# Attention and two expert layers on one core: first batch with S placed by a mask on VectorE, the queries behind the keys, the sums over 64 value columns, and the first slot's products by token halves

## The chip, the cores and the metric

The kernel runs on 1 core of one Trainium2 chip. The metric is the time of one execution in device microseconds (us), taken as the median of several runs. The engines are TensorE (PE; its weight loads are listed apart as PEld), VectorE (DVE), ScalarE (ACT), GpSimd (POOL), and SyncE (SP), which issues nearly all transfers. Each engine works through its own instructions strictly in order. An instruction waits until its operands are written and until the place it writes to has been read, and everything behind it on the same engine waits with it.

## What is computed

The reference, cut to what matters (4 batches, 4 heads, 1088 tokens, 32 values per head):

```python
def phi(x):                                   # 8 x 8 = 64 features of a row
    a = np.einsum('rd,bhsd->bhsr', S1, x)
    b = np.einsum('rd,bhsd->bhsr', S2, x)
    return np.einsum('bhsi,bhsj->bhsij', a, b).reshape(*x.shape[:-1], r * r)
q_p, k_p = phi(q), phi(k)
kv = np.einsum('bhsf,bhsd->bhfd', k_p, v);  z = np.sum(k_p, axis=2)
num = np.einsum('bhsf,bhfd->bhsd', q_p, kv)
den = np.einsum('bhsf,bhf->bhs', q_p, z)[..., None] + 1e-06
x = num / den                                 # 4352 tokens of 128
xn = x / rms * rms_g
g = xn @ w_gate                               # 128 -> 1536
x = (g / (1 + exp(-g)) * (xn @ w_val)) @ w_out
# then a soft mixture of 8 experts over all tokens: exp of x @ phi,
# sums over the tokens, 8 two-layer experts on 4 slots each, and back
```

The weights of the first expert layer and S1, S2 arrive as 64-bit floats; the kernel makes 32-bit words of them on the chip.

## The kernel before

**Stages.** A *front* works on batch 0 alone until the first 512 tokens (tile 0) are ready. Then 102 *slots* follow: tiles 0 to 7 have 512 tokens and 12 slots each, one for each 128 columns of the 1536; tile 8 has 6. The second expert layer and the way back make the end. Beside the slots run the key chains of batches 1 to 3, the query chain of the next tile and, in the first slots, the conversion of the weights.

**The front.** `FRONT` (L31 to L35) is an order written out by hand: each token names a step, and `in_order` (L872) holds each step's instructions behind the earlier ones of the same engine. The tokens that matter here:
- `n:18` and so on: fillers on TensorE (`keep_busy`, L301), products of a constant tile `hot` that nothing reads.
- `b`: `make_bd` (L260) makes words of S1 and S2 (tile `w4`, four copies side by side, by an add on POOL, L207), turns them with one TensorE transpose (L268), and copies the four blocks to the block diagonal `bd` with four ACT copies (L270). `bd` is the moving operand of every projection.
- `kt:0`, `kt:1`: key transposes on DVE, two halves each (L341). `kp`: projections of the keys (L359). `kt:2`, `kc:2`, `kp:2`: the same for the last 64 tokens.
- `qs`, `qp`: the query transpose on DVE (L506) and the query projection (L511), standing between the keys' first and last steps.
- `kx`, `ko`: the two halves of a projection are taken out of PSUM on ACT (L282, L279), and their outer products made on DVE or POOL (L287).
- `kv`: the values go to `va`, 33 columns a head with a column of ones (L352, ACT).
- `ks`: the sums over the tokens (L389): for each pair of heads a *bank* of 18 products with 33 columns of `va` as weights, which gives the rows 0 to 32 and 64 to 96 of a PSUM bank.
- `kw`: two copies of 33 rows for each bank to `kvT` (L407), spread four times; the rows between were zeroed once (L168). `kb`: transposes of it (L417). `kl`: placing them in `kvz` (L434). `qa` and after: attention, division, scaling by the root (L534 to L588), the transpose of the tokens (L594), and `xh` and `xl`, high and low part, by halves of 256 tokens (L601, L607).
- `c:0`, `c:1`, `c:2`: the next step of the conversion of a piece of the weights. Pieces 0, 1, 3, 4, 6 and 7 hold 256 columns each of gate and value weights and serve two slots; pieces 2, 5 and 8 hold output weights. The steps of a piece: absolute value (ACT, L192), shift (DVE, L194), low part (ACT, L198), join (DVE, L200), add (POOL, L204, two halves); then the high part `wgh` (ACT, L242) and the low part `wgl` (POOL, L249, two halves; of piece 0 on DVE, L251).

**A slot.** `ff_in` makes gate `g` and value `v` for 128 columns, each from three products of 512 tokens (`xh` by `wgh`, `xl` by `wgh`, `xh` by `wgl`; L647, L649, L648 in `mm3`). ACT takes silu of `g` (L677), DVE multiplies by `v` (L678, to `hh` in tile 0), and two slots later `ff_out` adds the product with the output weights to `o` (L702). `g` and `v` have two PSUM buffers each, so a slot waits until the slot two before it was read. The order within the slots is set by the scheduler of the language by its own costs, not by hand. `gate` holds the name of a product of the newest slot; transfers of the next batch wait for it.

## Time and profile before

| what | us |
|---|---|
| three runs, median (lowest, highest) | 316.48 (315.41, 316.87) |
| the profiled execution | 315.62 |
| its span, first to last instruction | 313.8 |
| outside the span | 1.82 |
| PE busy | 305.0 (97%) |
| DVE, ACT, POOL busy | 234.2, 181.4, 62.7 |

The page of the profile gives busy times over the whole span. An engine's share there says little of a change at one place, so the rows below come from the first 35 us. Fillers count as busy.

### The profile page before, as it was taken

The page shows a single profiled execution, that of the slowest core. Times are in us where ns is not written, and L with a number is a line of the kernel's source. Part 1 is how long each engine was busy: PE and PEld are TensorE (multiplying, and loading weights), DVE is VectorE, ACT ScalarE, POOL GpSimd, SP SyncE. Part 2 cuts the span into 40 slices and gives each one's busy share as a digit, 9 for nine tenths or more (in the row PEclk, how much of TensorE's full clock was granted, in tenths as well). Part 3 has the DMA queues.
Part 4 walks back from the last instruction along what each step waited for, and adds up shares of the span by engine and source line. Part 5 has one row for each costly group of instructions (what it writes and reads, how often), then busy time and mean ns, then how long its engine had stood idle before and what let it go on. Part 6 is the DMA issues. An engine that isn't in the chain of part 4 may idle for free.

```text
span 313.8 us, 5571 instructions
## 1 busy us (share of the span) xinstructions
PE 305.0 (97%) x1987; PEld 243.0 (77%) x1987; DVE 234.2 (75%) x454; ACT 181.4 (58%) x411; POOL 62.7 (20%) x104
## 2 busy tenths in 40 slices
PE   8989999999999999999999999999999999999993
PEld 6776676778888878888888788888787778898473
DVE  3787976688789858967798689678787667664673
ACT  3768674456645467555644676555574655567542
POOL 3347999000521010020010100100020100003030
PEclk9999999999999999999999999999999999999999
DMA  7998000010026100010261000100891493000007
GB/s 194 282 337 214 1 0 1 10 23 4 0 85 138 25 2 0 9 26 0 84 140 22 3 0 10 25 0 11 293 260 26 140 301 95 2 0 2 3 3 282
DMA packets 44955, 23.97 MB, mean 76 GB/s; under 512 B 26880, under 2 KB 40960, under 8 KB 44928
## 3 DMA queue, kind: packets, MB, share of 16 engines
q1 hardware_dynamic: 44752, 23.56, 27.7%
q8 instruction: 15, 0.25, 0.3%
q10 hardware_dynamic: 176, 0.07, 0.1%
q14 instruction: 12, 0.10, 0.1%
HBM read 19.81 MB, written 2.23 MB: 70 GB/s over the span
## 4 chain that ended last, share of the span: by engine, by line
PE 89%; DVE 2%; SPq 2%; POOL 2%; DMA 1%; issue 1%; ACT 1%; DVEq 0%; POOLq 0%; ACTq 0%
PE v L647 8%; PE g L647 8%; PE g L649 8%; PE g L648 7%; PE v L648 7%; PE v L649 7%; PE o L649 7%; PE o L647 7%; PE o L648 7%; PE aux L534 4%; PE o L702 3%; PE aux L389 2%; SPq L76 2%; PE aux L359 2%; PE aux L511 2%; PE fo L1207 1%
## 5 line engine op out<-in xcount | busy, mean ns | idle before, releaser
L677 ACT ACTIVATE silu<-g 128x512 f32<-128x512 f32 (+1 forms) x103 | 60.6, 593 | 38.0 <-PE g L649 37.3
L687 ACT CAST hh<-hf 128x512 fp32r<-128x512 f32 x89 | 54.8, 617 | 45.3 <-DVE hf L678 43.5
L678 DVE TENSOR_TENSOR hf<-v,silu 128x512 f32<-128x512 f32 (+1 forms) x91 | 61.1, 677 | 23.3 <-ACT hh L687 7.8
L692 DVE TENSOR_TENSOR hl<-hf,hh 128x512 fp32r<-128x512 f32 x89 | 61.0, 687 | 13.6 <-ACT hh L687 12.5
L647 PE MATMUL g<-xh,wgh 128*128 128x512 f32 (+1 forms) x108 | 43.8, 407 | 1.0 <-ACT xh L601 0.6
L647 PE MATMUL v<-xh,wgh 128*128 128x512 f32 (+1 forms) x108 | 43.4, 402 | 0.0
L648 PE MATMUL g<-xh,wgl 128*128 128x512 f32 (+1 forms) x108 | 41.1, 380 | 0.5 <-POOL wgl L249 0.5
L649 PE MATMUL g<-xl,wgh 128*128 128x512 f32 (+1 forms) x108 | 41.5, 384 | 0.0
L648 PE MATMUL v<-xh,wgl 128*128 128x512 f32 (+1 forms) x108 | 41.4, 383 | 0.0
L649 PE MATMUL v<-xl,wgh 128*128 128x512 f32 (+1 forms) x108 | 40.9, 379 | 0.0
L647 PE MATMUL o<-hh,woh 128*128 128x512 f32 (+1 forms) x94 | 36.9, 393 | 0.0
L649 PE MATMUL o<-hl,woh 128*128 128x512 f32 (+1 forms) x94 | 36.8, 392 | 0.0
L648 PE MATMUL o<-hh,wol 128*128 128x512 f32 (+1 forms) x94 | 35.8, 381 | 0.0
L582 POOL TENSOR_SCALAR rs<-ss 128x4 f32<-128x4 f32 (+1 forms) x8 | 1.9, 241 | 143.0 <-ACT sq L575 142.9
L647 PEld LDWEIGHTS g<-xh,wgh 128*128 128x128 f32 x108 | 20.4, 189 | 6.6 <-ACT silu L677 1.5
L648 PEld LDWEIGHTS g<-xh,wgl 128*128 128x128 f32 x108 | 20.3, 188 | 4.9 <-POOL wgl L249 0.9
L647 PEld LDWEIGHTS v<-xh,wgh 128*128 128x128 f32 x108 | 20.4, 188 | 4.3 <-issue 1.1
L649 PEld LDWEIGHTS g<-xl,wgh 128*128 128x128 f32 x108 | 20.3, 188 | 4.0
L648 PEld LDWEIGHTS v<-xh,wgl 128*128 128x128 f32 x108 | 20.4, 189 | 3.9 <-issue 0.7
L649 PEld LDWEIGHTS v<-xl,wgh 128*128 128x128 f32 x108 | 20.3, 188 | 3.9 <-issue 0.2
L649 PEld LDWEIGHTS o<-hl,woh 128*128 128x128 f32 x94 | 17.7, 188 | 3.7 <-issue 0.8
L647 PEld LDWEIGHTS o<-hh,woh 128*128 128x128 f32 x94 | 17.7, 188 | 3.4 <-issue 0.4
(263 smaller groups left out, 512.4 us busy)
## 6 DMA issues: line engine op xcount, KB each, us to landing
ring<-in_moe_w_dram SPq DMA_DIRECT2D x12, 256.0 KB, 6.9
ring<-in_moe_w_dram SPq DMA_DIRECT2D x5, 512.0 KB, 5.2
ring<-in_k_dram SPq DMA_DIRECT2D x8, 256.0 KB, 3.0
qt<-in_q_dram SPq DMA_DIRECT2D x4, 512.0 KB, 5.4
ring<-in_v_dram SPq DMA_DIRECT2D x16, 128.0 KB, 4.8
ring<-in_moe_w_gate_dram SPq DMA_DIRECT2D x6, 256.0 KB, 5.7
ring<-in_moe_w_val_dram SPq DMA_DIRECT2D x6, 256.0 KB, 7.1
ring<-in_moe_w_out_dram SPq DMA_DIRECT2D x3, 512.0 KB, 7.3
```

Source lines behind the costliest of these rows:

```text
L76: i = (on or nc.sync).dma_start(out=out, in_=in_)
L359: pe.matmul(o, self.kT[g][:, P * t : P * t + pp], bdf, start=True, stop=True)
L389: pe.matmul(self.a["kv", hp][64 * h2 : 64 * h2 + D1, 64 * hp : 64 * hp + 64], va[:, h, 2 * i + g, :] if t < 8 else vr[:, h, :], self.pk[hp ...
L534: pe.matmul(o, pD[:, f, h, :], rhs, start=(f == 0), stop=(f == 1))
L647: first = pe.matmul(o, ah, bh, start=start, stop=False)
L648: pe.matmul(o, al, bh, start=False, stop=False)
L649: last = pe.matmul(o, ah, bl, start=False, stop=stop)
L677: mark["silu"] = act.activation(s[:, cs], g[:, cs], AF.Silu).ins
L678: mark["gate"] = mark["gate", T, f] = dve.tensor_tensor(out=hf32[T, f][:, cs], in0=v[:, cs], in1=s[:, cs], op=ALU.mult).ins
L687: act.copy(hh[T, f], hf32[T, f])
L692: dve.tensor_tensor(out=hl[T, f], in0=hf32.pop((T, f)), in1=hh[T, f].bitcast(F32), op=ALU.subtract)
L702: last = pe.matmul(ops[T][:, 0:w], w_c, h[:, cs], start=(c == 0), stop=(c == NF - 1))
```

## The change

- **Placing S.** The four-fold `w4` is gone; the add of this step is made on DVE. Four TensorE products with the identity put the turned S into the four quarters of a PSUM tile. A new step `bm` (`place_bd`) multiplies it, read four times over, by a mask `blk` into all of `bd` in one DVE instruction. It stands between the two halves of `kt:0`. POOL makes the mask (five small memsets) in place of zeroing `bd`.
- **Order of the front.** `kp:2` is ahead of `qs` and `qp`; three fillers and two conversion steps ahead of the sums' results move: the low part of piece 0 (`c:0`, ACT) goes behind `kl`, and its `wgl` on DVE ahead of the scaling (`qm`).
- **Sums over 64 columns.** The weights of a sum are 64 columns of `va` (which gets a tail of 31 zeros) in place of 33. So the rows 0 to 127 of the bank are written, and one copy of 97 rows takes the place of two of 33, in the front and in the later batches; zeroing `kvT` is gone.
- **The first slot.** Its products with `xh` are made for tokens 0 to 255 first (high and low weights, `g` and `v`), then for 256 to 511, then both products with `xl` whole. `gate` keeps the first product of this slot.

```diff
-n:18 b n:5 kz kt:0 kt:1 qs kp:0 kp:1 kt:2 kx:0:a ko:0:d kx:1:b ko:1:p kc:2 qp kp:2 n:3 kv:0 kx:2:a ko:2:d qh kv:1 km
-ks:0 c:0 qo:0 qo:1 qb c:0 c:0 ks:1 kw:0:a kb:0 kw:1:a n:4 kb:1 n:10 kl:0:a kl:1:d c:0 c:0 kr:a c:1
-qa:0 qa:1 n:26 qd:0 qd:1 c:0 qq:0:a qq:1:d qq:2:a qq:3:d qr:0 qr:1 c:1 qm:0 qm:1 c:1 c:0 qt:0 qx:0 n:2 qt:1 qx:1 c:1 ql c:1 c:2 c:2 c:2
+n:18 b n:5 kz kt:0:0 bm kt:0:1 kt:1 kp:0 kp:1 kt:2 kx:0:a ko:0:d kx:1:b ko:1:p kc:2 kp:2 qs qp kv:0 kx:2:a ko:2:d qh kv:1 km
+ks:0 c:0 qo:0 qo:1 qb c:0 ks:1 kw:0:a kb:0 kw:1:a n:4 kb:1 n:10 kl:0:a kl:1:d c:0 c:0 c:0 kr:a c:1
+qa:0 qa:1 n:26 qd:0 qd:1 c:0 qq:0:a qq:1:d qq:2:a qq:3:d qr:0 qr:1 c:0 qm:0 qm:1 c:1 c:1 qt:0 qx:0 n:2 qt:1 qx:1 c:1 ql c:1 c:2 c:2 c:2
...
-        if len(out.shape) == 2:
+        if out.shape[1] == D:
+            dve.tensor_tensor(out=out, in0=s, in1=r, op=ALU.add)
...
-        pe.transpose(a[:, 0 : 2 * R], w4.rearrange("p h d -> p (h d)"), ident[0 : 2 * R, 0 : 2 * R])
-        for h in range(4):
-            act.copy(bd[32 * h : 32 * h + 32, h, :], a[32 * h : 32 * h + 32, 0 : 2 * R])
+        for h in range(H):
+            pe.matmul(a[32 * h : 32 * h + 32, 0 : 2 * R], w, ident[0 : 2 * R, 0 : 2 * R], start=True, stop=True)
+        kt["S"] = a
+
+    def place_bd():
+        a = kt.pop("S")[:, 0 : 2 * R].unsqueeze(1).to_broadcast([P, H, 2 * R])
+        dve.tensor_tensor(out=bd, in0=a, in1=blk.unsqueeze(2).to_broadcast([P, H, 2 * R]), op=ALU.mult)
...
-                        self.a["kv", hp][64 * h2 : 64 * h2 + D1, 64 * hp : 64 * hp + 64],
-                        va[:, h, 2 * i + g, :] if t < 8 else vr[:, h, :],
+                        self.a["kv", hp][64 * h2 : 64 * h2 + 64, 64 * hp : 64 * hp + 64],
+                        (va_all if t < 8 else vr_all)[:, v0 : v0 + 64],
...
-            for h2 in range(2):
-                r0 = 64 * h2
-                src = self.a["kv", hp][r0 : r0 + D1, 64 * hp : 64 * hp + 64].rearrange("p (a n) -> p a n", n=D)
-                eng(kvT[r0 : r0 + D1, 2 * hp : 2 * hp + 2], src.unsqueeze(2).to_broadcast([D1, 2, 4, D]))
+            src = self.a["kv", hp][0:97, 64 * hp : 64 * hp + 64].rearrange("p (a n) -> p a n", n=D)
+            eng(kvT[:, 2 * hp : 2 * hp + 2], src.unsqueeze(2).to_broadcast([97, 2, 4, D]))
...
+        if (T, f) == (0, 0):
+            os, sl = (gps[T, f][0], vps[T, f][0]), slice(0, P)
+            for cs in cuts(512):
+                for w_m in (wgh, wgl):
+                    for m, o in enumerate(os):
+                        last = pe.matmul(o[:, cs], w_m[:, m, sl], xh[T][:, cs], start=(w_m is wgh and cs.start == 0), stop=False)
+                        gate[0] = gate[0] or last.ins.name
+            for m, o in enumerate(os):
+                last = pe.matmul(o, wgh[:, m, sl], xl[T], start=False, stop=True)
```

The line numbers in the orders of after are those of the changed file (L198, L204, L206, L212 are the conversion steps L192, L198, L200, L204 of before).

TensorE, from the key projections to the sums. Before (`x_192` is the transposed queries, `T` the transposed keys; each filler has a load of `hot` and a product):

```order
L344 MATMUL v<-ident,kr 128x64
L511 MATMUL aux<-bd,x_192 128x64 x4
L359 MATMUL g<-bd,T 64x64
L301 LDWEIGHTS hot
L301 MATMUL idle<-hot 128x256
...
L389 MATMUL v<-work,va 33x64 x16
L389 MATMUL v<-pkr,vr 33x64 x2
```

After:

```order
L353 MATMUL v<-ident,kr 128x64
L368 MATMUL aux<-bd,T 64x64
L517 MATMUL g<-bd,x_220 128x64 x4
L399 MATMUL v<-work,va 64x64 x16
L399 MATMUL v<-pkr,vr 64x64 x2
```

The query projection now stands directly ahead of the sums, and the fillers there are gone.

ACT, after the low part of piece 1 (of the weights of slots 2 and 3) in the first slots. Before:

```order
L601 ACTIVATE xh<-v,g_sb 128x256
L192 ACTIVATE ring<-ring 128x512
L198 ACTIVATE cvc<-ring 128x512
L242 CAST wgh<-cvt 128x2x256
L677 ACTIVATE silu<-g 128x512
L192 ACTIVATE hf<-ring 128x512
L198 ACTIVATE cvc<-ring 128x512
L192 ACTIVATE hf<-ring 128x512
L677 ACTIVATE silu<-g 128x512 x2
```

After:

```order
L607 ACTIVATE xh<-v,g_sb 128x256
L198 ACTIVATE ring<-ring 128x512
L204 ACTIVATE cvc<-ring 128x512
L694 ACTIVATE silu<-g 128x512
L198 ACTIVATE hf<-ring 128x512 x2
L247 CAST wgh<-cvt 128x2x256
L204 ACTIVATE cvc<-ring 128x512
L694 ACTIVATE silu<-g 128x512
```

The cast that slot 2 needs moved behind the first silu and two absolute values of later pieces.

POOL, the conversion in the first slots (`cvt` is piece 1, `ring` output weights, `hf` pieces 3 and 4). Before:

```order
L204 TENSOR_TENSOR cvt<-cvs,cvc 128x256 x2
L249 TENSOR_TENSOR wgl<-cvt,wgh 128x256 x2
L204 TENSOR_TENSOR ring<-cvs,cvc 128x256 x2
L204 TENSOR_TENSOR hf<-cvs,cvc 128x256 x4
L249 TENSOR_TENSOR wgl<-hf,wgh 128x256 x4
```

After:

```order
L212 TENSOR_TENSOR cvt<-cvs,cvc 128x256 x2
L212 TENSOR_TENSOR ring<-cvs,cvc 128x256 x2
L254 TENSOR_TENSOR wgl<-cvt,wgh 128x256 x2
L212 TENSOR_TENSOR hf<-cvs,cvc 128x256 x4
L254 TENSOR_TENSOR wgl<-hf,wgh 128x256 x2
L212 TENSOR_TENSOR ring<-cvs,cvc 128x256 x2
L254 TENSOR_TENSOR wgl<-hf,wgh 128x256 x2
```

The output weights went ahead of the low part that slots 2 and 3 need.

## Rows read from the trace of the kernel before

**Rows 1.** Windows: length, then busy us (instructions) of each engine, granted clock, DMA.

```profile
22.65:34.20 11.55, 10.60 (x42) 6.79 (x42) 9.77 (x18) 9.23 (x18) 9.22 (x12) 1.00 0.62 152
34.20:290.00 255.80, 255.80 (x1569) 207.70 (x1573) 196.74 (x361) 149.03 (x331) 41.36 (x66) 1.00 0.21 53
```

**Rows 2.** Timeline of PE, 5 us: start, duration, engine, line, tiles, count.

```profile
5.17 0.28 PE L268 MATMUL aux<-ident,csr 16*128 16x16 f32 x1
5.39 1.24 PE L301 MATMUL idle<-hot 128*128 128x256 bf16 x5
6.43 0.25 PE L359 MATMUL aux<-bd,T 128*128 128x64 f32 x1
```

**Rows 3.** Timeline of ACT in the front; in brackets the idle time before.

```profile
5.49 0.69 ACT L270 COPY bd<-aux 32x16 f32<-32x16 f32 x4 [1.31 <-PE aux L268]
7.50 0.27 ACT L282 COPY asb<-aux 128x128 f32<-128x128 f32 x1 [1.32 <-PE aux L359]
...
12.07 0.66 ACT L198 ACTIVATE cvc<-ring 128x512 uint32<-128x512 uint32 x1
...
13.39 0.74 ACT L407 COPY kvT<-aux 33x256 f32<-33x256 f32 x2
```

**Rows 4.** Timeline of DVE in the front: key transposes, query transpose, first outer product.

```profile
4.41 2.01 DVE L341 STREAM_TRANSPOSE T<-ring 128x256 f32<-128x256 f32 x4
7.48 0.71 DVE L506 STREAM_TRANSPOSE x<-qt 128x512 f32<-128x512 f32 x1 [1.06 <-DMA qt<-in_q_dram]
8.12 1.18 DVE L287 TENSOR_TENSOR work<-asb,aux 128x1024 f32<-128x1024 f32 x1
```

**Rows 5.** Timeline of PE: query projection and the two banks of sums.

```profile
8.49 1.10 PE L511 MATMUL aux<-bd,x 128*128 128x64 f32 x8
...
10.22 1.09 PE L389 MATMUL v<-work,va 128*33 128x64 f32 x32
...
12.49 0.30 PE L389 MATMUL aux<-pkr,vr 64*33 64x64 f32 x4
```

**Rows 6.** Groups by line and form, weight loads: busy us, mean ns, idle before.

```profile
L389 PEld LDWEIGHTS aux<-work,va 128*33 128x33 f32 x224 | 6.5, 111 | 1.7 <-issue 1.3
L541 PEld LDWEIGHTS aux<-kvr,work 128*64 128x64 f32 x16 | 1.3, 136 | 0.7 <-issue 0.7
```

**Rows 7.** Timeline of ACT at the start of the slots.

```profile
21.45 0.48 ACT L601 ACTIVATE xh<-g,g_sb 128x256 fp32r<-128x256 f32 x1 [1.42 <-PE g L594]
22.13 0.47 ACT L601 ACTIVATE xh<-v,g_sb 128x256 fp32r<-128x256 f32 x1 [0.20 <-PE v L594]
...
24.53 0.62 ACT L242 CAST wgh<-cvt 128x512 fp32r<-128x512 f32 x1 [0.81 <-POOL cvt L204]
...
25.55 0.67 ACT L192 ACTIVATE hf<-ring 128x512 f32<-128x512 f32 x1
```

**Rows 8.** Timeline of PE: first products of slots 0 and 2, output of slot 0, a wait.

```profile
22.65 0.50 PE L647 MATMUL g<-xh,wgh 128*128 128x512 f32 x1 [0.56 <-ACT xh L601]
...
25.70 0.50 PE L647 MATMUL g<-xh,wgh 128*128 128x512 f32 x1
...
28.68 1.02 PE L702 MATMUL o<-hh,ring 128*128 128x512 f32 x2
...
34.20 0.50 PE L648 MATMUL g<-xh,wgl 128*128 128x512 f32 x1 [0.50 <-POOL wgl L249]
```

**Rows 9.** Timeline of POOL: conversion in the first slots.

```profile
25.23 1.45 POOL L249 TENSOR_TENSOR wgl<-cvt,wgh 128x256 fp32r<-128x256 f32 x2 [0.73 <-ACT wgh L242]
27.31 1.79 POOL L204 TENSOR_TENSOR ring<-cvs,cvc 128x256 uint32<-128x256 uint32 x2 [0.63 <-DVE cvs L200]
29.84 3.62 POOL L204 TENSOR_TENSOR hf<-cvs,cvc 128x256 uint32<-128x256 uint32 x4 [0.74 <-DVE cvs L200]
```

**Rows 10.** Timeline of DVE: product of slot 0, join of the output weights.

```profile
25.68 0.69 DVE L678 TENSOR_TENSOR hh<-v,silu 128x512 f32<-128x512 f32 x1 [1.78 <-PE v L649]
26.29 0.94 DVE L200 SCALAR_TENSOR_TENSOR cvs<-ring 128x512 uint32<-128x512 uint32 x1
```

More of the change, by code (lines that the diff above doesn't have):

```diff
@@ L161, in body @@
     bd = const.tile([P, H, 2 * R], F32, name="bd")
-    pool.memset(bd, 0.0)
+    blk = const.tile([P, H], F32, name="blk")
+    pool.memset(blk, 0.0)
+    for h in range(H):
+        pool.memset(blk[32 * h : 32 * h + 32, h : h + 1], 1.0)
     pool.memset(va[:, :, :, D:D1], 1.0)
     pool.memset(vr[:, :, D:D1], 1.0)
+    pool.memset(va_all[:, H * 8 * D1 :], 0.0)
+    pool.memset(vr_all[:, H * D1 :], 0.0)
     mhalf = const.tile([P, 4], F32, name="mhalf")
@@ L167, in body @@
     kvT = const.tile([97, 4, 4, D], F32, name="kvT")
-    pool.memset(kvT[32:64], 0.0)
     kvr = const.tile([P, 2, H, 4, D1], F32, name="kvr")
@@ L201, in f64_words @@
         yield
-        if len(out.shape) == 2:
+        if out.shape[1] == D:
+            dve.tensor_tensor(out=out, in0=s, in1=r, op=ALU.add)
+        else:
             for c in cuts(out.shape[1]):
                 mark["word"] = pool.tensor_tensor(out=out[:, c], in0=s[:, c], in1=r[:, c], op=ALU.add).ins
-        else:
-            s, r = (x.unsqueeze(1).to_broadcast(out.shape) for x in (s, r))
-            pool.tensor_tensor(out=out, in0=s, in1=r, op=ALU.add)
         yield
@@ L332, in size, with transpose @@
             return (4, P) if g < 2 else (1, 64)
-        def transpose(self, g):
-            self.kT[g] = row("T", 2)
+        def transpose(self, g, es=range(2)):
+            if 0 in es:
+                self.kT[g] = row("T", 2)
             if g < 2:
-                for e in range(2):
+                for e in es:
                     src = kt[self.b][:, 2 * g : 2 * g + 2, :, e, :].rearrange("p h j d -> p (h j) d")
@@ L397, in spread @@
         def spread(self):
-            for h2 in range(2):
-                r0 = 64 * h2
-                src = self.a["kv"][r0 : r0 + D1, 0:128].rearrange("p (a n) -> p a n", n=D)
-                act.copy(kvT[r0 : r0 + D1], src.unsqueeze(2).to_broadcast([D1, 4, 4, D]))
+            src = self.a["kv"][0:97, 0:128].rearrange("p (a n) -> p a n", n=D)
+            act.copy(kvT, src.unsqueeze(2).to_broadcast([97, 4, 4, D]))
         def spread_1(self, hp, eng):
-            for h2 in range(2):
-                r0 = 64 * h2
-                src = self.a["kv", hp][r0 : r0 + D1, 64 * hp : 64 * hp + 64].rearrange("p (a n) -> p a n", n=D)
-                eng(kvT[r0 : r0 + D1, 2 * hp : 2 * hp + 2], src.unsqueeze(2).to_broadcast([D1, 2, 4, D]))
+            src = self.a["kv", hp][0:97, 64 * hp : 64 * hp + 64].rearrange("p (a n) -> p a n", n=D)
+            eng(kvT[:, 2 * hp : 2 * hp + 2], src.unsqueeze(2).to_broadcast([97, 2, 4, D]))
         def back(self, ids=range(4), banks=1):
@@ L893, in front @@
             "b": make_bd,
+            "bm": place_bd,
             "kz": k.zero,
-            "kt": lambda g: k.transpose(int(g)),
+            "kt": lambda g, e=None: k.transpose(int(g), range(2) if e is None else [int(e)]),
             "kc": lambda g: k.copy(int(g)),
```

13 lines of the change are left out of this document (9 added, 4 removed).

## The prediction, made before the changed kernel was run

> **What bounds the kernel now.** I read the stretches first. From 34.2 to 290 us TensorE is busy for all of 255.8 us, and from 22.65 to 34.2 for 10.60 of 11.55 us [rows 1]. So after 34.2 nothing that the change moves on another engine can shorten the time, unless the products themselves change; what can be won is when TensorE starts on tile 0, and how long it waits until 34.2, where its last wait is for a low part from POOL [rows 8]. Then I read the timelines of the first 35 us, engine by engine, because a step of the front that is not last costs nothing. The granted clock is 1.00 in both stretches [rows 1], so it takes part in no term.
>
> **Placing S: no gain, 0.1 us lost.** The four ACT copies to `bd` end at 5.49 + 0.69 = 6.18 [rows 3], but the first projection starts at 6.43, when the five fillers ahead of it are through: they start at 5.39 and take 1.04 / 5 = 0.21 each [rows 2]. The copies are hidden by 0.25 us of fillers, so taking them away gives nothing. Four products take the place of one that held TensorE from 5.17 to 5.39 [rows 2], and the fillers wait behind them. The trace has no such product of 16 rows in a quarter. At best the fillers start 0.1 us earlier, as the add no longer goes through POOL's queue; at worst each further product costs 0.22, which is 0.66 later. Nearest are the sums, where 32 instructions take about 1.0 us, 0.03 each [rows 5]: seven more of those are 0.2. I take 0.1 later, between -0.1 and +0.3 for the range. The mask multiply on DVE replaces the copies; it waits for the products, about 5.6, and takes at most 0.3, so it ends near 5.9, under the same fillers. Behind it stand three of the four key transposes, which end at 6.42 now [rows 4]; they would end near 7.5, and TensorE reads the last of them about 1.4 us after the first projection starts, near 7.9. That cover of 0.4 us is what the step rests on. POOL's five memsets lie in its idle first microseconds.
>
> **Queries behind the keys, one copy for two.** Today the first outer product starts at 8.12, because the query transpose (7.48 to 8.19) is ahead of it on DVE [rows 4], though its operand is there at 7.50 + 0.27 = 7.77 [rows 3]. After: 7.92 with the 0.1 lost above, ended at 9.10. The query transpose (0.71) then ends at 9.8, and the query projection (1.10 for eight instructions [rows 5]) runs from 9.85 to 10.85, now directly ahead of the sums on TensorE. So the sums start at 10.85 and not 10.22 [rows 5]: 0.63 **later**. Two banks take 12.49 + 0.30 - 10.22 = 2.57 [rows 5] and end at 13.42. What was late until now was ACT: its low part of piece 0 (12.07, 0.66) stands ahead of four copies, and the last two end at 13.39 + 0.74 = 14.13 [rows 3]. With the low part behind and one copy of 0.37 for each bank (the same 256 columns; a copy's length here goes by columns), the last copy runs from 13.50 to 13.87. Gain: 14.13 - 13.87 = 0.26 us. So most of what ACT gives up, TensorE takes by the queries. The bounds of the first step make it 0.05 to 0.45. The low part behind the placing on ACT is needed by POOL only after the join on DVE, which also stands behind the placing; it stays hidden. The copies saved in the later batches are on ACT, which is busy for 149 of 255.8 us there [rows 1]: nothing.
>
> **64 columns.** As many products, on as many streamed columns; only the weight loads grow by 31 columns. A load of 33 columns is recorded with 111 ns, one of 64 with 136 ns [rows 6]: 25 ns more. If the load hides behind the product of the other half of the array, as loads of 33 do, the price is nothing; if it stands on TensorE's path, it is 25 ns for each of 72 loads in the first batch (1.8 us) and 216 in the later ones (5.4 us). I take nothing: 32 instructions of both halves pass in 1.0 us [rows 5], 0.03 each, far less than the 0.11 of one recorded load, so loads do lie beside other work. The other end is a rival below. The Trainium skill has a rule on each side: "TensorE: Matmul & The Clock Gate", section "LDWEIGHTS (loading the stationary operand)", lets a load grow with its columns, 1/1.2 ns each, so 26 ns for 31, and the recorded 25 ns agree; "TensorEngine Tiling (Array Packing)", section "Key Properties", lets separate tiles load and multiply in parallel. By the first alone the sum would be the rival's, by the second it stays as it is, and no row of before settles it.
>
> **The first slot.** The halves of `xh` are ready at 21.93 and 22.60, and TensorE starts at 22.65, after the second [rows 7, 8]. Twelve products of two slots take until 25.70 [rows 8], about 0.24 each. Of the first slot's four products with `xh` (0.96 us), half (0.48) now run between the two arrivals, which are 0.67 apart: 0.48 gained. With the 0.26 from above, slots 0 and 1 are through at about 24.8 in place of 25.6. Transfers of the next batch start about 1.3 us earlier; they use no engine that waits here.
>
> **Where this is lost and given back.** Slot 2 needs the cast of piece 1. Now it runs at 24.53 to 25.15, and slot 2 starts at 25.70 [rows 7, 8]. In the new order of ACT it stands behind silu of slot 0, which cannot start before about 23.75 (gate of slot 0 is complete after ten products), and behind two absolute values: 0.5 (silu, from 25.15 to 25.55 with its overlap) + 2 x 0.57 (0.67 less 0.1 overlap) + 0.62 [rows 7], so it ends at 26.0, and slot 2 starts at 26.05. TensorE waits 1.25 us; the whole lead is gone there, and 0.35 more. After that the new order has more to do between waits: two products of slot 2 (to 26.5); the output product of slot 0, which needs silu (24.3), 0.69 and 0.94 on DVE [rows 10] and half of 1.79 on POOL [rows 9], so 26.8; 0.86 for it (1.02 less the tail [rows 8]), 0.9 query projection, two products 0.46, another output product 0.86: 29.9. The low part of piece 1 follows on POOL, 25.9 + 1.79 + 1.45 [rows 9] = 29.15, in time. Eight products: 31.7. Slot 4 waits for its buffer: words of piece 3 (29.15 + 3.62 / 2 = 30.95), cast (0.62) and silu (0.5) end at 32.1, so it starts at 32.15. Before, TensorE at 34.20 [rows 8] had done more than this by one output product (0.86) and three products (0.69): the comparable point is 32.15 + 1.55 = 33.70. **Gain 34.20 - 33.70 = 0.5 us.** Behind that, POOL is about 1.5 us ahead of the order of before, so I expect no new wait, and TensorE's work is the same.
>
> **The sum.** Profiled execution 315.62 - 0.5 = 315.1; it lies 0.86 under the median, so on the median 316.48 - 0.5 = 316.0. The gain's own range is -0.3 (one more wait of 0.8) to 1.3 (the words of piece 3 at 0.73 a half, a low front): 315.2 to 316.8.
>
> **Rivals.**
> *The lead is carried whole.* If the cast comes when its words are there and no later, the 0.26 and the 0.48 stay, and of the 0.95 us that TensorE waits between 22.65 and 34.2 [rows 1] most goes, as the new order has other work at hand: 0.74 + 0.9 = 1.6, 314.9. Against it stands ACT's order, which is fixed.
> *The wider loads stand on the path.* This one is slower: 7.2 us by the loads above, less the 0.5: 323.2. It decides where a load of 64 columns outlasts the product that it hides behind. For it speaks that the recorded load grows; against it that loads pass at 0.03.
> *A new wait.* In the new order output product and low part are one chain over ACT, DVE and POOL; were POOL's pieces 0.3 longer each over five pieces, 1.5 us, the time would be 316.48 + 1.0 = 317.5.
>
> **Chances.** Forecast 0.65, whole lead 0.16, wider loads 0.10, new wait 0.09. The range of 8 in 10 leaves out the wider loads and half of the two small cases' ends: 314.6 to 317.3. About 0.5%, 1.6 us, is what a measurement of this kernel can tell from no change. Faster by more: half of the whole lead and an edge of the forecast with it, 0.15. Slower by more: the wider loads and a little of the new wait, 0.12. Within: 0.73.
>
> **What the changed profile would show.** The first projection at 6.4 to 6.7, not earlier. The sums start near 10.85, and two banks take 2.6, not 4.4. The last copy to `kvT` ends near 13.9. First products 0.7 to 0.8 us before 22.65. A wait of over 1 us ahead of slot 2, ended by the cast on ACT; a short one ahead of slot 4. From about 33 on no wait of TensorE. It would be wrong if the sums' pairs pass slower than now, if fillers do not bind the first projection, or if the cast is not what slot 2 waits for.

## The result, and the profile after

The change made the kernel slower by 0.54%: 317.4 us median of 20 runs (316.38 to 322.86) against 315.73 of the kernel before, timed again beside it; ratio 1.0054, interval 1.0031 to 1.0078. A second measurement (e9 below) gave 1.0055 (1.0037 to 1.0074). The forecast was 316.0 with 314.6 to 317.3: it missed both the time and the side. As a change it was 0.5 us less, reckoned from the 316.48 then on record; measured are 1.67 us more, reckoned from 315.73. The runs of the changed kernel fall into two groups: in 22 of 31 it took 316.4 to 318.8, in 9 it took 320.2 to 322.9 at a mean granted clock of 0.988 to 0.978. (The ratios leave out the executions above 321 as disturbed, though here the kernel itself brings them about, so they rather understate the loss.)

The profiled execution (320.18, span 318.1) is one of the 9. Its windows of the front (columns: length, busy us of PE, PEld, DVE, ACT and POOL with instructions, granted clock, DMA share, GB/s):

```profile
8.00:10.00 2.00, 1.19 (x9) 0.85 (x8) 2.00 (x3) 1.08 (x4) 0.95 (x1) 1.00 1.12 281
10.00:12.00 2.00, 2.00 (x18) 1.88 (x20) 0.28 (x2) 0.44 (x2) 2.00 (x3) 0.57 0.96 281
...
14.00:16.00 2.00, 2.00 (x36) 1.85 (x34) 0.73 (x2) 0.26 (x1) 0.00 (x0) 0.50 1.04 384
16.00:18.00 2.00, 2.00 (x18) 1.66 (x15) 0.32 (x2) 0.79 (x3) 0.00 (x0) 0.72 1.08 389
```

The granted clock falls to 0.50, the level of 1.2 GHz, at about 10 us and is back at 1.00 (2.4 GHz) at about 17; before, it was 1.00 throughout. Ahead of the fall TensorE was busy for 1.19 of 2 us. The timeline of PE (start, duration, line, count; in brackets the idle time before a row) shows what that does:

```profile
9.13 0.33 PE L368 MATMUL aux<-bd,T 128*64 128x64 f32 x2 [0.37 <-ACT T L356]
9.90 1.63 PE L517 MATMUL g<-bd,x 128*128 128x64 f32 x8 [0.43 <-DVE x L512]
11.46 1.98 PE L399 MATMUL v<-work,va 128*64 128x64 f32 x32
...
15.68 0.48 PE L399 MATMUL aux<-pkr,vr 64*64 64x64 f32 x4
...
24.56 0.41 PE L600 MATMUL g<-ident,x 128*128 128x128 f32 x2 [0.94 <-DVE x L594]
...
25.54 0.39 PE L678 MATMUL g<-xh,wgh 128*128 128x256 f32 x1
...
29.96 0.50 PE L653 MATMUL g<-xh,wgh 128*128 128x512 f32 x1 [1.17 <-ACT wgh L247]
```

The query projection takes 1.63 and not 1.10 [rows 5], and the two banks of sums 4.70 (11.46 to 16.16) instead of 2.57. The two waits ahead of that, 0.37 and 0.43, stand ahead of the last key projection and ahead of the query projection; before, TensorE had no wait here, and three fillers between the last key projection and the sums.

To see the rest of the change without the clock, the same kernel must be read in an execution where the clock holds. Run e9 (the changed kernel again, 317.3 in its profiled execution, clock 1.00 from 8 to 18 us) is one:

```profile
6.00 1.09 PE L368 MATMUL aux<-bd,T 128*128 128x64 f32 x8
...
8.59 0.33 PE L368 MATMUL aux<-bd,T 128*64 128x64 f32 x2 [0.37 <-ACT T L356]
9.33 1.10 PE L517 MATMUL g<-bd,x 128*128 128x64 f32 x8 [0.41 <-DVE x L512]
10.36 1.27 PE L399 MATMUL v<-work,va 128*64 128x64 f32 x32
...
12.91 0.33 PE L399 MATMUL aux<-pkr,vr 64*64 64x64 f32 x4
...
21.17 0.41 PE L600 MATMUL g<-ident,x 128*128 128x128 f32 x2 [0.94 <-DVE x L594]
...
22.14 0.39 PE L678 MATMUL g<-xh,wgh 128*128 128x256 f32 x1
...
26.56 0.50 PE L653 MATMUL g<-xh,wgh 128*128 128x512 f32 x1 [1.16 <-ACT wgh L247]
...
32.95 0.50 PE L653 MATMUL g<-xh,wgh 128*128 128x512 f32 x1 [0.57 <-ACT silu L694]
...
296.59 0.66 PE L1152 MATMUL aux<-ident,work 128*128 128x128 f32 x4 [0.17 <-DVE work L1145]
```

The last copy to `kvT` in e9, on ACT:

```profile
13.29 0.37 ACT L413 COPY kvT<-aux 97x256 f32<-97x256 f32 x1 [0.97 <-PE aux L399]
```

Two rows of before, as landmarks (transposes of the tokens, and the same wait in the tail):

```profile
21.00 0.41 PE L594 MATMUL g<-ident,x 128*128 128x128 f32 x2 [0.38 <-DVE x L588]
...
295.79 0.65 PE L1134 MATMUL aux<-ident,work 128*128 128x128 f32 x4 [0.16 <-DVE work L1127]
```

The first projection starts at 6.43 before, at 6.45 in the profiled execution after and at 6.00 in e9; that moment scatters with the start of an execution (see the end), so places are compared behind it (the forecast's own places behind its 6.53). Shift against before in us, later is positive:

| place | predicted | e9, clock 1.00 | profiled after |
|---|---|---|---|
| sums start | +0.53 | +0.57 | +1.22 |
| last copy to kvT ends | -0.36 | -0.04 | +2.42 |
| transposes of the tokens | -0.36 | +0.60 | +3.54 |
| first product of slot 0 | -0.84 | -0.08 | +2.87 |
| slot 2 | +0.25 | +1.29 | +4.24 |
| slot 4, comparable point | -0.60 | +0.73 | not worked out |
| landmark in the tail | -0.60 | +1.23 | +4.20 |

(The comparable point is the prediction's: slot 4 plus 1.55 against 34.20 before, [rows 8].) So there are two losses: about 1.2 us in an execution in which the clock holds, and 3.0 more (4.20 less 1.23) in this one, where it fell. e9's span is 1.7 longer than that of before (315.5 against 313.8): 1.23, less 0.43 for the earlier first projection, and 0.9 behind the tail's landmark (18.9 against 18.0). That last stretch takes 18.0 to 19.6 in the eighteen traces, in kernels with and without the change, so the 0.9 is not tied to it.

### The profile page after: what moved, and what is told of

Its sections match the earlier page's. It is cut to its first block, busy times and chain, and to the rows that moved or that the text cites. A ratio compares the mean times of both kernels' runs of the same rounds, so it can differ in the third digit from the quotient of the medians.

```text
span 318.1 us, 5591 instructions
## 1 busy us (share of the span) xinstructions
PE 307.8 (97%) x1995; PEld 247.1 (78%) x1995; DVE 234.8 (74%) x456; ACT 179.4 (56%) x402; POOL 61.5 (19%) x108
## 4 chain that ended last, share of the span: by engine, by line
PE 89%; DVE 3%; POOL 2%; DMA 2%; issue 1%; ACT 1%; SPq 0%; DVEq 0%; POOLq 0%; ACTq 0%
PE g L653 7%; PE v L653 7%; PE g L654 7%; PE v L654 7%; PE v L655 7%; PE g L655 7%; PE o L655 7%; PE o L653 7%; PE o L654 6%; PE aux L540 4%; PE aux L399 3%; PE o L719 3%; PE aux L368 2%; PE idle L309 2%; PE aux L517 2%; DMA kr<-in_k_dram 2%
## 5 line engine op out<-in xcount | busy, mean ns | idle before, releaser
L695 DVE TENSOR_TENSOR hf<-v,silu 128x512 f32<-128x512 f32 (+1 forms) x91 | 61.3, 679 | 18.9 <-PE v L655 9.0
L653 PE MATMUL g<-xh,wgh 128*128 128x512 f32 (+1 forms) x107 | 44.7, 417 | 2.0 <-ACT wgh L247 1.2
L653 PE MATMUL v<-xh,wgh 128*128 128x512 f32 (+1 forms) x107 | 41.9, 392 | 0.0
L655 PE MATMUL g<-xl,wgh 128*128 128x512 f32 (+1 forms) x107 | 40.5, 379 | 0.0
```

What stands on the lines that cost most here:

```text
L653: first = pe.matmul(o, ah, bh, start=start, stop=False)
L655: last = pe.matmul(o, ah, bl, start=False, stop=stop)
L695: mark["gate"] = mark["gate", T, f] = dve.tensor_tensor(out=hf32[T, f][:, cs], in0=v[:, cs], in1=s[:, cs], op=ALU.mult).ins
```

## Experiments on the clock

Each run below gives the ratio to the kernel before, timed beside it on the same chip, with its interval.

**e1, four fillers more in the changed kernel.** Two in each of the two idle stretches:

```diff
-kc:2 kp:2 qs qp kv:0
+kc:2 n:2 kp:2 n:2 qs qp kv:0
```

> The changed kernel with four fillers more on TensorE: two ahead of the last key projection (kp:2) and two ahead of the query projection (qp), where TensorE stood idle for 0.37 and 0.43 us in the trace after, just before the granted clock fell to 0.5. Nothing else differs. Theory A (the idle stretches left by the three fillers that were taken out let the clock fall, and all of TensorE's work until 17 us then passes at half speed): granted clock 1.00 from 8 to 18 us in every run, query projection about 1.1 us instead of 1.63, two banks of sums about 2.7 us instead of 4.7, first product of slot 0 near 22.5 instead of 25.5, time 316.6, as in those runs of the changed kernel whose mean clock was 1.00. Theory B (the sums with 64 columns themselves bring the clock down): clock still 0.5 in the sums, time 317.4, single runs at 320.

Measured: 317.41 against 316.34, ratio 1.0044 (1.0026 to 1.0062); 12 runs from 316.88 to 318.44, none at 320. The two idle stretches are gone and the clock reads 1.00 (timeline of PE, then a window):

```profile
8.12 0.39 PE L309 MATMUL idle<-hot 128*128 128x256 bf16 x2
...
8.82 0.39 PE L309 MATMUL idle<-hot 128*128 128x256 bf16 x2
9.30 1.10 PE L517 MATMUL g<-bd,x 128*128 128x64 f32 x8
```

```profile
10.00:12.00 2.00, 2.00 (x46) 1.80 (x47) 1.26 (x2) 1.51 (x4) 1.48 (x2) 1.00 0.90 292
```

Theory A holds for the clock: with the same sums over 64 columns it stays up. Its time, 316.6, did not come; that theory B's 317.4 did is chance, as B's cause was not there. What stays is a steady loss of 1.07 us by the medians while the clock holds. It is the greater part of the 1.67 that the medians show for the change; the falls cost 3 us or more each, but come in less than a third of the executions.

**e9, the changed kernel again.**

> The changed kernel itself once more, on the chip of the next three. Theory A (in it the clock falls in the front of some executions, in others not): single runs at 320 or more with a mean clock of 0.988 or less, which no run of e1 to e8 showed, beside runs of 316.4 to 317.5; median about before + 1.5. Theory B (the falls of the clock belonged to the chip of the first measurement): no run at 320, median as e1, before + 1.1.

Measured: 317.65 against 315.88; 9 runs from 316.98 to 318.8, two at 321.88 and 322.86 (mean clock 0.980 and 0.978). Theory A. The profiled execution has the same two waits as the one above (0.37 and 0.41), TensorE was busy for 1.22 of the 2 us from 8 to 10, and the clock held: the idle stretches allow the fall, they don't force it.

**e13 and e14, one of the two stretches filled**, the first in e13, the second in e14:

```diff
-kc:2 kp:2 qs qp kv:0
+kc:2 n:2 kp:2 qs qp kv:0
```

```diff
-kc:2 kp:2 qs qp kv:0
+kc:2 kp:2 n:2 qs qp kv:0
```

> The changed kernel with two fillers in the first idle stretch only (ahead of kp:2), the second (0.43 us ahead of qp) left. Theory A (both stretches together let the clock fall; half of the idle time is too little): no run at 320 or over, median as e1, before + 1.1. Theory B (the second stretch alone does it): some of 12 runs at 320 or over, as in the changed kernel (9 of 31 so far at 0.988 or less).

> The changed kernel with two fillers in the second idle stretch only (ahead of qp), the first (0.37 us ahead of kp:2) left. Theory A: no run at 320 or over, median as e1, before + 1.1. Theory B (the first stretch alone does it): some of 12 runs at 320 or over.

Measured: e13, 317.4 against 316.2, ratio 1.0042 (1.0014 to 1.0069), 3 of 12 runs at 320.58 to 322.08. e14, 320.62, ratio 1.0071 (1.0029 to 1.0112), 5 of 9 runs at 320.62 to 322.3. Theory B in both: either stretch alone is enough for falls in some executions. In e14's profiled execution the fall comes behind one wait of 0.37 and lasts from 10 to beyond 20 us (timeline, then windows):

```profile
9.01 0.33 PE L368 MATMUL aux<-bd,T 128*64 128x64 f32 x2 [0.37 <-ACT T L356]
...
9.78 1.75 PE L517 MATMUL g<-bd,x 128*128 128x64 f32 x8
```

```profile
10.00:12.00 2.00, 2.00 (x18) 1.88 (x19) 0.15 (x2) 0.44 (x2) 1.94 (x2) 0.51 0.98 260
...
18.00:20.00 2.00, 2.00 (x12) 1.50 (x11) 1.81 (x5) 1.91 (x7) 0.00 (x0) 0.50 1.06 389
20.00:22.00 2.00, 2.00 (x18) 1.97 (x18) 0.79 (x3) 1.62 (x5) 1.42 (x2) 0.93 1.01 343
```

**e15, the kernel before without its three fillers.**

```diff
-kc:2 qp kp:2 n:3 kv:0
+kc:2 qp kp:2 kv:0
```

> The kernel before without the three fillers behind kp:2, nothing else. There the sums start at 10.22 and the last key projection ends at 9.9, so that TensorE would stand idle for at most 0.3 us in place of 0.8. Theory A (it is the idle time, not the missing fillers as such, that lets the clock fall): clock 1.00 in the sums, time as before. Theory B (the three fillers are needed wherever the work stands): some runs 3 us or more above the others at a mean clock of 0.988 or less.

Measured: 315.49 against 316.2, ratio 0.9987 (0.9971 to 1.0002), 12 runs from 315.22 to 316.82. Theory A: it is the idle time, not the fillers as such. With the query projection ahead of the last key projection there is no wait to fill; the sums start at once, at 9.75 in place of 10.22 [rows 5], with the first projection at 6.42 and 6.43:

```profile
9.75 0.30 PE L389 MATMUL v<-work,va 128*33 128x64 f32 x2
```

So the three fillers cost the kernel before 0.47 us at the sums, and in 12 runs without them the clock did not fall, while the new order needs its own. By counts: with both stretches filled (e1, e2, e3, e5, e7) 0 of 51 runs were at 320 or more; with one or none filled 17 of 52. No run of any other kernel here reached 320 either. One comes near: a run of e10 (below, the front of before with the wider sums) at 319.02 with a mean clock of 0.988, 2.8 above its median. It was not traced, and the mean does not tell where a clock fell: in e4 (below) 0.989 stands for a fall behind the slots. So it stays open whether the wider sums alone can bring a fall in the front. Nor is it known what decides from run to run: in the two traced falls the first projection started at 6.45, in e9 and e13, where the clock held, at 6.00 and 6.34, which is too few to go by.

## Experiments on the front

**e5, sums over 33 columns and two copies again** (on e2, see below; `spread` and the zeroing of `kvT` as before, too):

```diff
-                        self.a["kv", hp][64 * h2 : 64 * h2 + 64, 64 * hp : 64 * hp + 64],
-                        (va_all if t < 8 else vr_all)[:, v0 : v0 + 64],
+                        self.a["kv", hp][64 * h2 : 64 * h2 + D1, 64 * hp : 64 * hp + 64],
+                        va[:, h, 2 * i + g, :] if t < 8 else vr[:, h, :],
```

> As e2_fill_scale, but the sums take 33 columns of the values again, in the front and in the later batches, and two copies of 33 rows take the place of one of 97. Theory A (a load of 64 columns costs about 0.15 us for a bank of 36 even at full clock): two banks of the first batch 2.43 us instead of 2.73, the three later batches together 0.57 less, one copy of 0.37 more on ACT's path; the end 0.5 us earlier than in e2, which is before + 0.5. Theory B (my prediction's term, wider loads cost nothing): banks as in e2, the end as in e2 or, by the second copy, 0.4 later: before + 1.1 to + 1.4.

**e10, the kernel before with sums over 64 columns and one copy**, nothing else: the lines of the diff above the other way round, and the tail of `va`, `spread` and `spread_1` of the change.

> The kernel before with the sums over 64 columns and one copy of 97 rows, nothing else of the change (the scheduler's order in later slots moves a little). Theory A (64 columns cost 0.15 us a bank at full clock): two banks of the first batch 2.7 us instead of 2.43, the later six 0.57 together, one copy of 0.37 less on ACT in the front; the end 0.3 to 0.6 later, before + 0.5; granted clock 1.00 in the sums, so that the wider sums alone do not lower it. Theory B (my prediction's term): no difference or 0.3 faster.

Measured: e5, 317.35 against 316.08, ratio 1.0040 (1.0024 to 1.0056), no gain against e2's 1.0040. e10, 316.2 against 315.88, ratio 1.0017 (0.9996 to 1.0038). The times settle nothing at this size: e5's speaks for theory B, e10's interval holds both. The banks in the traces are as theory A says. Two banks of the first batch take 2.58 us in e5, as before, 2.75 in e10 (10.10 to 12.85) and 2.88 in e9 (10.36 to 13.24). In a later batch, timeline of PE, after (64 columns) and then before (33):

```profile
69.43 1.15 PE L399 MATMUL aux<-work,va 128*64 128x64 f32 x32
...
70.78 1.15 PE L399 MATMUL aux<-work,va 128*64 128x64 f32 x32
```

```profile
63.08 1.09 PE L389 MATMUL aux<-work,va 128*33 128x64 f32 x32
...
64.33 0.50 PE L647 MATMUL o<-hh,woh 128*128 128x512 f32 x1
```

A bank takes 1.35 (69.43 to 70.78) instead of 1.25 (63.08 to 64.33). That is 0.17 us in the first batch of e10 and 0.3 in that of e9, where the query projection stands directly ahead (2 and 4 ns a load, 72 loads), and 6 x 0.1 = 0.6 in the later ones (3 ns a load, 216 loads): 0.8 to 0.9 in all, neither the 0 of the forecast nor the 7.2 of the rival with its 25 ns a load. The 0.6 is read from the length of the banks; farther on it shows only in part. From slot 0 to the tail's landmark, kernels with the first slot whole take 273.1 to 273.4 us with 33 columns (before, e11, e15) and 273.9 to 274.0 with 64 (e3, e10), but with the slot by halves e5's 274.8 with 33 is no less than the 274.3 to 274.5 of e1, e6, e9 and e13 with 64. Of the two rules that the prediction cited, the trace is nearer to the one of the Trainium skill's page "TensorEngine Tiling (Array Packing)", section "Key Properties", by which separate tiles load and multiply in parallel.

**e6, queries ahead again** (on e2, with the fillers of the kernel before):

```diff
-kt:1 kp:0 ... kc:2 n:2 kp:2 n:2 qs qp kv:0
+kt:1 qs kp:0 ... kc:2 qp kp:2 n:3 kv:0
```

> As e2_fill_scale, but the query transpose stands ahead of the first outer product on DVE and the query projection ahead of the last key projection on TensorE, with three fillers behind it, all as in the kernel before (instead of the four fillers of e1). Theory A (the queries behind the keys delay the sums by a whole projection): sums 3.8 us behind the first projection instead of 4.3 to 4.5, slot 0 and the end 0.5 us earlier than in e2, before + 0.5; clock 1.00 in the front. Theory B (another step takes the time, as the outer products come later by the transpose): sums and end as in e2, before + 1.0.

Measured: 316.43 against 316.08, ratio 1.0018 (1.0005 to 1.0031), 12 runs at 315.9 to 316.92, none at 320. The sums start 3.90 behind the first projection (e9: 4.36), and the ratio is 0.22% under e2's, 0.7 us. Theory A. By this the queries behind the keys are the largest single loss of the front, and they are the one from which the idle stretches come; but the intervals of e6 and e2 overlap, and e12 below, with the queries in the same place, is at 1.0034. What is firmer comes with e16.

**e2, the low part of piece 0 behind the scalings**, and **e12, the shift of piece 1 behind them too.** e2 is e1 with the first of these edits, e12 is e6 with the second:

```diff
-qr:0 qr:1 c:0 qm:0 qm:1 c:1 c:1 qt:0
+qr:0 qr:1 c:1 qm:0 qm:1 c:1 c:0 qt:0
```

```diff
-qr:0 qr:1 c:1 qm:0 qm:1 c:1 c:0 qt:0
+qr:0 qr:1 qm:0 qm:1 c:1 c:1 c:0 qt:0
```

> As e1_fill, and on DVE the low part of piece 0 (L256, 0.68 us) stands behind the two scalings again, as in the kernel before, instead of ahead of them. Theory A (the scaling was late because DVE was at the low part): TensorE's wait ahead of the transposes of the tokens (L600) falls from 0.9 to about 0.4, slot 0 starts 0.5 earlier than in e1_fill and the end comes 0.5 earlier: 316.1. Theory B (slot 2 waits for a cast whose chain does not hang on the scaling, so that the lead is waited away there): slot 0 0.5 earlier, the end as in e1_fill, 316.6.

> As e6_queries_ahead, and on DVE the shift of piece 1 (0.42 us) stands behind the two scalings too. Theory A (POOL's root, 0.73 us in before, takes 0.96 with that shift begun just before it and 1.22 with the low part, because POOL is held while that DVE instruction runs): the first root takes 0.73 again, TensorE waits 0.4 ahead of L600 instead of 0.7, the end 0.25 earlier than in e6. Theory B (POOL's longer time is its own or modelled): root and wait as in e6.

Measured: e2, 317.36, ratio 1.0040 (1.0021 to 1.0059), as e1. e12, 317.06 against 315.88, ratio 1.0034 (1.0017 to 1.0051), no better than e6. The mechanism shows in the traces. In e9, DVE's low part (L256) begins just ahead of POOL's first root, and the scaling (L594) waits for the root; DVE, then POOL:

```profile
19.03 0.36 DVE L588 TENSOR_SCALAR rs<-ss 128x2 f32<-128x2 f32 x2
19.30 0.69 DVE L256 TENSOR_TENSOR wgl<-cvt,wgh 128x512 fp32r<-128x512 f32 x1
20.59 0.42 DVE L594 TENSOR_TENSOR x<-x,rs 128x256 f32<-128x256 f32 x1 [0.61 <-POOL rs L589]
```

```profile
19.34 1.90 POOL L589 TENSOR_TENSOR rs<-rs,mhalf 128x2 f32<-128x2 f32 x2 [1.56 <-DVE rs L588]
```

In e12 nothing of the conversion stands between:

```profile
18.35 0.36 DVE L588 TENSOR_SCALAR rs<-ss 128x2 f32<-128x2 f32 x2
19.42 0.43 DVE L594 TENSOR_TENSOR x<-x,rs 128x256 f32<-128x256 f32 x1 [0.71 <-POOL rs L589]
```

```profile
18.66 1.40 POOL L589 TENSOR_TENSOR rs<-rs,mhalf 128x2 f32<-128x2 f32 x2 [1.56 <-DVE rs L588]
```

Two roots take 1.90 in the first case and 1.40 in the second; the first one alone takes 1.23 and 0.72, and 0.96 in e2, where the shorter shift begins just ahead of it. TensorE's wait for the scaling is 0.94, 0.45 and 0.68. So POOL's instruction was held while a DVE instruction that had begun first was running. The Trainium skill, page "SBUF — State Buffer", section "SBUF: two separate sides", has this rule: of a GpSimd instruction and a VectorE one that needs the port pair they share, the one that starts first gets it whole and the other waits. The trace agrees where the VectorE instruction is first, with 0.5 us of hold, of the 0.65 for which the low part still ran. Where the root is first, the other half of that rule does not show. In before it began 0.03 ahead of the shift; POOL, then DVE:

```profile
19.67 1.40 POOL L583 TENSOR_TENSOR rs<-rs,mhalf 128x2 f32<-128x2 f32 x2 [1.50 <-DVE rs L582]
```

```profile
19.70 0.45 DVE L194 TENSOR_SCALAR cvt<-cvt 128x512 uint32<-128x512 uint32 x1
```

In e10, with the same order of instructions, the root began 0.05 behind the shift; DVE, then POOL:

```profile
18.90 0.42 DVE L197 TENSOR_SCALAR cvt<-cvt 128x512 uint32<-128x512 uint32 x1
```

```profile
18.95 1.64 POOL L583 TENSOR_TENSOR rs<-rs,mhalf 128x2 f32<-128x2 f32 x2 [1.56 <-DVE rs L582]
```

The shift takes 0.45 behind a root of 0.73 and 0.42 ahead of one, so it hardly waits; the first root takes 0.73 in before and 0.96 in e10. With it goes TensorE's wait: 0.38 or 0.39 in all seven traces with sums over 33 columns, 0.68 in all five with 64 columns and the shift in this place (e2, e3, e6, e7, e10). The traces with 64 columns have one semaphore instruction more on POOL's queue ahead of the root, 17 ns long, and the others have none. So of the 0.56 by which e9's wait is longer than that of before, 0.30 came with the wider sums and 0.26 with the low part.

For the time, e2 went as theory B says; e12 went as neither, with root and wait as theory A has them and nothing of it at the end: its ratio is above e6's. Of the 0.26 that e2 wins here, and of e12's 0.2, nothing reaches the end. In e12 slot 2 waits 1.18 for its cast as before and starts 4.82 behind slot 0 (4.46 in e6), since the words of piece 1 now begin later. In e2's execution a wait that is 0.2 in e9 took more than was won:

```profile
PE aux L353 <- DMA kr<-in_k_dram: 0.8, 1, 0.8
```

**e11, the kernel before with the mask and with the low part behind the placing** (`make_bd`, `place_bd` and `blk` of the change, and in `FRONT`):

```diff
-kz kt:0 kt:1 qs ... qb c:0 c:0 ks:1 ... kl:1:d c:0 c:0 kr:a
+kz kt:0:0 bm kt:0:1 kt:1 qs ... qb c:0 ks:1 ... kl:1:d c:0 c:0 c:0 kr:a
```

> The kernel before with S placed by the mask and with the low part of piece 0 on ACT behind the placing (kl); queries, sums, scaling and slots as before. Theory A: where the fillers pass at 0.11 us each, the copies to bd bound the first projection (they did in e8: copies ended 5.83, fillers 5.57, projection 5.88), so the mask wins 0.2 to 0.3 there, and the copies to kvT no longer wait for the low part, 0.3: the end 0.4 to 0.5 earlier than before. Theory B (my prediction: fillers bind, nothing from the mask, 0.1 lost, 0.3 from the copies): 0.2 earlier at most.

Measured: 316.1 against 315.88, ratio 1.0006 (0.9992 to 1.0020): theory B, no gain that can be measured. Where the fillers pass in 0.11 us, the ACT copies do bind: in e8, with the copies, the first projection starts 0.85 behind the start of the five fillers, and in e5, with the mask, 0.56, which is when they are through:

```profile
5.03 0.72 PE L303 MATMUL idle<-hot 128*128 128x256 bf16 x5
5.88 1.10 PE L361 MATMUL aux<-bd,T 128*128 128x64 f32 x8
```

```profile
5.05 0.72 PE L310 MATMUL idle<-hot 128*128 128x256 bf16 x5
5.61 1.13 PE L369 MATMUL aux<-bd,T 128*128 128x64 f32 x8
```

That lead does not reach the sums. e11's first projection is 0.48 ahead of e8's (5.40 against 5.88), but its sums start at 9.71 against 9.73: in e11 the query transpose waited 0.47 and the values' copy 0.55 for loads.

## Experiments on the first slots

**e4, the kernel before with the halves alone, and e3, which is e2 without them.** The edit is the piece of `ff_in` that begins with this line, put in for e4 and taken out for e3:

```diff
+        if (T, f) == (0, 0):
```

> The kernel before with the first slot's products by token halves and nothing else of the change. The scheduler's order on ACT behind it is the one of the changed kernel (cast of piece 1 behind silu and two absolute values). Theory A: slot 0 starts 0.6 us earlier (22.0 instead of 22.65), slot 2 waits over 1 us for the cast, the end 0.5 us later: 316.2. Theory B (prediction): the wait at slot 2 is won back by 34 us, the end 0.5 us earlier, 315.2.

> As e2_fill_scale, but the first slot's products are made over all 512 tokens again, in the order of the kernel before; with that the scheduler puts the cast of piece 1 on ACT ahead of silu of slot 0 again. Theory A (the halves win 0.65 us at slot 0 and the order that they bring on ACT loses 1.2 at slot 2, with nothing given back later): slot 0 0.65 later than in e2, no wait over 0.3 us ahead of slot 2, the end 0.5 earlier than in e2: 315.6. Theory B (my prediction's term: behind slot 2 the new order wins it back): the end 0.5 later than in e2, 316.6.

Measured: e4, 317.09 against 316.34, ratio 1.0033 (1.0012 to 1.0054); e3, 317.53, ratio 1.0041 (1.0021 to 1.0062), as e2. The halves win what they should: from the transposes to slot 0 it is 0.97 us with them (e1, e2, e4, e9) and 1.65 without (before, e3), 0.68 earlier. Then slot 2 waits for the cast of piece 1, which the scheduler puts behind silu and two absolute values; ACT in e9:

```profile
24.29 0.60 ACT L694 ACTIVATE silu<-g 128x512 f32<-128x512 f32 x1 [0.40 <-PE g L681]
24.79 1.22 ACT L198 ACTIVATE hf<-ring 128x512 f32<-128x512 f32 x2
25.89 0.62 ACT L247 CAST wgh<-cvt 128x512 fp32r<-128x512 f32 x1
```

From slot 0 to slot 2 it is 4.4 to 4.5 us with the halves and 3.05 without: 1.4 lost for 0.68 won. About 0.6 of this comes back by slot 4 in e9. e4 is slower, as theory A says, but its trace does not explain by how much: at the first product of slot 101 its profiled execution is level with before (275.7 and 275.8 behind the first projection). Three of its 12 runs have a mean clock of 0.989; in the profiled one of them the clock fell behind the slots, and why it does so there is open:

```profile
290.00:295.00 5.00, 5.00 (x49) 2.71 (x42) 1.56 (x9) 1.61 (x6) 0.00 (x0) 0.75 0.02 3
```

In e3, theory A's 0.5 us did not come, nor did theory B's.

**e7 and e8, the cast first.** e2, and e4, with the absolute values of later pieces held behind the cast of piece 1:

```diff
-        with paced():
+        with paced(), tc.issue_after(mark["cast"]) if "cast" in mark else nullcontext():
             act.activation(t, hi.bitcast(F32), AF.Abs, scale=2.0 ** -112)
...
-            act.copy(dh, src)
+            last = act.copy(dh, src)
+        if key == ("gv", 1):
+            mark["cast"] = last.ins
```

> As e2_fill_scale, with one order more: the absolute values of later pieces on ACT stand behind the cast of piece 1 (L247). The scheduler's order behind slot 2 changes with it. Theory A (slot 2 waits for that cast, and nothing behind it gives the 1.2 us back): TensorE's wait ahead of slot 2 falls from 1.2 to under 0.3, the end 1.0 us earlier than in e2: about the time before. Theory B (the lead is waited away at slot 4 or at a low part): a wait of about 1 us appears there, the end as in e2: before + 1.0.

> The kernel before with the first slot by token halves and with the cast of piece 1 ahead of the absolute values of later pieces on ACT; nothing else of the change. Theory A: slot 0 starts 0.68 us earlier relative to the last transposes, slot 2 waits under 0.3, the end 0.7 us earlier than before: 315.6 against 316.3. Theory B (the lead is waited away later): the time of before, 316.3.

Measured: e7, 317.74 against 316.08, ratio 1.0053 (1.0032 to 1.0074); e8, 316.11, ratio 1.0017 (0.9999 to 1.0036). The wait ahead of slot 2 is gone in both, and nothing is won: theory B. PE in e7:

```profile
25.05 0.50 PE L655 MATMUL g<-xh,wgh 128*128 128x512 f32 x1
...
27.02 0.50 PE L656 MATMUL v<-xh,wgl 128*128 128x512 f32 x1 [0.42 <-POOL wgl L256]
```

Slot 2 starts 19.28 behind the first projection, 1.0 earlier than in e2, and then waits for the low part of the same piece on POOL, for a transpose on DVE (0.17), and in several places for 0.1 us. From the start of slot 2 to the first product of slot 101 it takes 258.0 us in e7, 256.3 in e1 and 256.5 before. The cast was one link; behind it stand the words and low parts on POOL.

**e16, what had shown an earlier landmark put together** on the kernel before: e11 and e8.

> What showed an earlier landmark in its trace, put together on the kernel before: S by the mask, low part of piece 0 behind the placing, first slot by halves, cast of piece 1 ahead of later absolute values. Theory A (e8 and e11 each hide a gain of 0.2 to 0.3 under the scatter, and they add): 0.5 earlier than before. Theory B (the chain of conversion behind slot 2 sets the time, so what is won ahead of it is waited away): the time of before, within 0.3.

Measured: 316.28 against 316.2, ratio 1.0005 (0.9990 to 1.0020): theory B. It differs from e7 in two things alone: the queries are ahead again, with the fillers of before, and the sums take 33 columns. e7's ratio is 1.0053 (1.0032 to 1.0074), and the intervals lie apart. So the steady loss lies in these two steps together, 0.48% or 1.5 us; how it splits between them (0.22% for the queries by e6, 0.17% for the columns by e10) is less sure. No kernel here beats the one before by more than its interval; e15, which only leaves out three fillers, is nearest.

## Why the prediction was wrong, point by point

- **Right.** The fillers bound the first projection (6.45 for a forecast 6.4 to 6.7; runs with faster fillers apart). The queries delayed the sums: 4.36 behind the first projection for a forecast 4.32. The halves won 0.68 for 0.48. Slot 2 waited 1.17 for the cast for a forecast 1.25, and a short wait stood ahead of slot 4.
- **The step that failed first: "The granted clock is 1.00 in both stretches, so it takes part in no term."** Those stretches began at 22.65. For the front, the text let the three fillers go without a price; it had TensorE's new wait for the query transpose only as a starting time, and the one for the transposed T not at all. With both of them filled no run of 51 was at 320 or more; with either left open 17 of 52 were, at 3 us or more each.
- **The steady loss, which makes up most of the median's miss.** At the tail e9 is 1.83 later than forecast (+1.23 for -0.60). By the table 0.32 of it is there at the last copy to `kvT`, 0.64 comes up to the transposes, the halves win 0.20 more than forecast, 0.28 comes at slot 2, 0.29 up to slot 4 and 0.50 behind it. The next points name the terms. By the times, the queries and the columns carry it (e16 against e7): the delay by the queries was forecast rightly (the sums +0.57 for +0.53), but the gains that were to outweigh it did not come or did not last.
- **"64 columns ... I take nothing."** By the length of the banks it was 0.2 to 0.3 in the first batch and about 0.6 later, and 0.3 more came by way of POOL's root (e10). The term's ends, 0 and 7.2, held it; the value taken was wrong. That 32 products pass in 1.0 us bounds the price of a hidden load, not of a wider one. With the 0.3, the one copy for two gains 0.04 in place of 0.26. Even that rests on the one execution of before that was read: there ACT had waited 0.71 us for a load ahead of its conversion, and the last copy ended 7.70 behind the first projection; in e4, which has the same front, it waited 0.22 and ended 7.28. The 0.2 that the first outer product was to win rests on the same execution: its query transpose had waited for its load until 7.48, while in e15, in the same place, it started at 6.79 and held nothing up.
- **The low part moved ahead of the scaling had no term at all.** It held POOL's root, for which the scaling waits, 0.26 us longer than the shift of before's order does (0.94 against 0.68). The description of the change named its place, and the prediction never asked what POOL did at that moment. That the root, which begins just ahead of the shift in before, would begin behind it with the wider sums, no row of before could show.
- **"Where this is lost and given back": behind slot 2 the forecast won 0.85 back to slot 4, and e9 won 0.56.** The waits named there were right; the size was off by 0.3, and another 0.5 was lost behind slot 4, near the 0.6 by which the later banks are longer.
- **The rivals.** The one that came nearest, a new wait with 317.5, has the time but not the mechanism: that is luck. None held the clock.

## What to carry to other kernels

Fillers that cover a wait are part of the time: before they are taken out, or the order around them changes, list the waits that TensorE then has, and price the work behind them at the lower clock as a case of its own. A VectorE instruction that begins just ahead of a GpSimd one on a critical chain can lengthen that one, by 0.23 and 0.5 us here, even if VectorE is idle there; which of the two begins first can hang on 0.05 us. Where a chain of conversion feeds the first slots, as here, a lead won ahead of it is waited away at its next link; shorten the chain, or leave the lead.

## What the runs showed of the hardware

- A fall of the granted clock to 0.50 can follow waits as short as 0.37 us in a stretch of small products. It is a matter of chance from run to run (9 of 31 executions of the same kernel) and in the two traced falls it lasted some 7 us (mean clock 0.988) and over 10 (0.979). The Trainium skill, page "TensorE: Matmul & The Clock Gate", section "A second HAM failure mode: psum-queue depth-cycling", tells of a kernel whose TensorE idles briefly and often between groups of products, so that its clock swings between its two levels. These runs agree in part: the waits are short and the clock falls, but one fall followed one or two waits, and no trace shows it swing to and fro.
- The first fillers of every execution pass in 0.21 us each, and from some moment on in 0.11, while the profile's granted clock reads 1.00 from the start. That moment was about 4.5 us in e5 and 6.4 in the profiled executions of before and after; the first projection lay between 5.40 and 6.45 in the eighteen traces. A single time carries this scatter, so small changes are read behind the first projection, as long as no load binds in between, as it did in e11.
- A load of 64 columns in place of 33, recorded with 25 ns more, cost 2 to 4 ns on TensorE's path.
- A POOL instruction that begins 0.04 to 0.05 us behind a VectorE one is held (0.96 for 0.73, with a shift of 0.42; 1.23 with a low part of 0.69). A VectorE shift that begins 0.03 behind the POOL one took 0.45 for 0.42.
